# Turning q and k for attention: eight TensorE transposes and two PSUM copies a group, or a transposing DMA

## The chip, the cores and the metric

The kernel runs on one core of one Trainium2 chip. The metric is the device time of one launch in microseconds (us). Every kernel's time below is a median of several runs; every ratio compares runs in the fast state alone. Engines are called PE (TensorE), PEld (its weight loads), DVE (VectorE), ACT (ScalarE), POOL (GpSimd) and SP (SyncE, which here only issues DMAs). "Clock" is the TensorE clock that was granted, as a share of full speed.

## The reference, cut to what matters

A gated linear attention with a complex decay, then a gated feed-forward layer:

```python
for t in range(S):                                   # B=4, H=8, S=768, D=48
    S_re, S_im = a_re*S_re - a_im*S_im + kv[t], a_re*S_im + a_im*S_re
    y[:, :, t] = einsum('bhd,bhde->bhe', q[:, :, t], S_re)
x = y as (3072 tokens, 384)
out = x + sigmoid(x @ w_res) * ((gelu(x @ w_gate) * (x @ w_val)) @ w_out)    # d_ff = 1536
```

The kernel does the recurrence in chunks of 128 tokens. The decay becomes a scaling and a rotation of q and k by an angle for each token and element, so that each head has 48 real and 48 imaginary columns: 96. Within a chunk the attention matrix is K Q^T, masked. For that matmul q and k must lie with the 96 columns on the partitions; they are computed with the tokens on the partitions. So they have to be turned, 128 tokens x 96 columns for each head. The change is about who turns them.

## The kernel before

There are 12 groups of 256 tokens (two chunks c each, three groups for one batch element), and six units u of two groups. A unit passes through two stages:

- the *preparing stage* (`phase_x`): logarithms, exponentials, arctan, then the sines and cosines CS of the angles fg, for the next units; output matmuls of the unit before; some attention;
- the *gelu stage* (`phase_y`): twelve blocks of gate and value matmuls (gp, vp) with their gelu, the rotations of q and k, and nearly all attention of the next unit.

ACT changes its function table at each boundary, so the boundaries can be read from its table loads. Within a stage a scheduler lays down one static order for each engine; each engine then runs its own list in order, and waits where an operand is not there.

The parts that the change touches, with cuts marked:

```python
pE  = tile_pool(bufs=2)          # E, Ei and the angles fg: two of each
pQ  = tile_pool(bufs=2)          # CS, and the rotated Q and K
psT = tile_pool(bufs=1, PSUM)    # transposes
psA = tile_pool(bufs=1, PSUM)    # attention matrix
# ... cut
def cs_t(g, c):
    if c == 0:
        T["fg", g] = pE.tile([128, C * H, 2, D], FP, tag="fg")
    # ... matmul cst, r = round(cst)                        (DVE)
    fg[:, hs, 1, :] = cst - r                             # (DVE, 0.54 us a chunk)
    if c == C - 1:
        fg[:, :, 0, :] = abs(fg[:, :, 1, :])              # (DVE, 0.95 us)

def p2_sin(g):
    CS[:, :, 0] = Sin(2 pi * fg[:, :, 0] + hpi)           # (ACT, 0.94 us)
    CS[:, :, 1] = Sin(2 pi * fg[:, :, 1])                 # (ACT, 0.83 us)

def mk(nm, src):                                          # rotation, nm is "Q" or "K"
    t = pQ.tile([128, C * H, 2, D], BF, tag=nm)
    nc.vector.tensor_tensor(out=t, in0=T["CS", g], in1=sb, op=OP.mult)
# ... cut
def grp(hg):                                              # four heads of one chunk
    tp = psT.tile([128, 1024], BF, tag="tp")
    for j in range(4): nc.tensor.transpose(out=tp[0:DD, j*128:j*128+128], in_=Q(x), identity=ident)
    for j in range(4): nc.tensor.transpose(out=tp[0:DD, 512+j*128:640+j*128], in_=K(x), identity=ident)
    nc.scalar.copy(out=qk[0:DD, 0:512], in_=tp[0:DD, 0:512])              # Q, ACT
    nc.vector.tensor_copy(out=qk[0:DD, 512:1024], in_=tp[0:DD, 512:1024]) # K, DVE
    at = psA.tile([128, 4, 128], FP, tag="at")
    for j in range(4): nc.tensor.matmul(out=at[:, j], lhsT=qk[.. K ..], rhs=qk[.. Q ..])
    nc.vector.tensor_tensor(out=atm, in0=at, in1=mask4, op=OP.mult)
```

All loads of a_re, a_im, q and k, and all stores, are issued by SP, one after the other.

## Time and profile before

| | before |
|---|---|
| time, median of 3 runs | 343.38 us (342.88 to 344.42) |
| span of the profiled run | 341.4 us |
| up to the first gelu stage | 94.0 us |
| four preparing stages / four gelu stages | 80.0 / 104.5 us |
| rest (last attention, last gelu stage, output) | 62.9 us |

From the page of the kernel before, the busy time of the engines, the granted clock in 40 slices (a digit is tenths), and the DMA queue that SP feeds (packets, MB, share of 16 engines):

```profile
PE 267.3 (78%) x2054; PEld 160.6 (47%) x2080; DVE 245.4 (72%) x440; ACT 203.0 (59%) x338; POOL 67.1 (20%) x104
...
PEclk9996585559699999999999999999999999999999
...
q1 hardware_dynamic: 103296, 23.60, 40.6%
```

PE is the busiest, but 78% is an average over stages with different limits. The table of busy time by stretch for the kernel before shows them. Each line is a stage: its window, its length, busy time of each engine (with the count of instructions), the granted clock, the DMA share and GB/s. The lines are the first gelu stage, the first preparing stage after it, and the third gelu stage. (The DMA share adds up the packets' times and can exceed 1, as the 1.26 below.)

```profile
core 0: us, PE busy (x) PEld busy (x) DVE busy (x) ACT busy (x) POOL busy (x), PEclk, DMA share, GB/s
94.02:120.00 25.98, 24.39 (x251) 15.67 (x254) 22.43 (x40) 16.34 (x31) 6.08 (x8) 1.00 1.26 166
120.00:140.79 20.79, 17.26 (x83) 9.65 (x83) 16.21 (x32) 17.13 (x28) 6.58 (x10) 1.00 0.94 156
...
187.23:213.84 26.61, 26.06 (x269) 16.79 (x271) 24.28 (x44) 16.80 (x31) 0.00 (x0) 1.00 0.28 53
```

In the gelu stages PE is busy 94 to 99% of the time at full clock, with DVE close behind. PE work removed there should count. In the preparing stage shown no engine is above 84%: it is limited by a chain of small steps. Note also the DMA share: over 1 in the first gelu stage, where the loads are still running, 0.28 in the third.

What turning costs, from the groups of instructions of the kernel before (line, engine, operation, operands, count, then busy us and mean ns of one, then idle time before them):

```profile
L322 ACT COPY qk<-tp 96x512 bf16<-96x512 bf16 x48 | 27.9, 581 | 28.3 <-PE tp L320 15.1
...
L317 PE MATMUL tp<-ident,Q 128*96 128x128 bf16 x192 | 20.1, 231 | 13.4 <-DVE qk L323 8.6
...
L323 DVE COPY qk<-tp 96x512 bf16<-96x512 bf16 x48 | 19.9, 414 | 10.1 <-ACT qk L322 9.6
L119 ACT ACTIVATE CS<-fg,hpi 128x768 bf16<-128x768 f32 x12 | 11.2, 935 | 24.1 <-DVE fg L237 24.1
```

The 231 ns of a transpose overlaps its neighbours. The timeline of PE in the kernel before gives the real cost (start in us, duration, then the instructions of one row):

```profile
201.20 0.38 PE L317 MATMUL tp<-ident,Q 128*96 128x128 bf16 x4
201.42 0.39 PE L320 MATMUL tp<-ident,K 128*96 128x128 bf16 x4
201.64 0.33 PE L426 MATMUL rp<-wr,xT 128*128 128x384 bf16 x1
```

Four transposes hold PE for 0.22 us from start to start, so a group of four heads (q and k) costs 0.44 us of PE, 0.58 us of ACT and 0.41 us of DVE. There are 48 such groups.

The last line of the groups: ACT's sines wait 24.1 us in all for fg.

### The profile page before, as it was taken

The numbers are of one execution on the slowest core, as the hardware profiler recorded it, in microseconds if no ns is written. First come the engines' busy times: TensorE is split into PE (matmuls) and PEld (weight loads), VectorE is DVE, ScalarE is ACT, GpSimd is POOL, SyncE is SP. The second block draws the span as 40 slices with busy tenths as digits, with TensorE's granted clock in tenths as the row PEclk, the third lists the DMA queues.
The fourth block names the chain that finished last, engine by engine and source line by source line (L and its number), as shares of the span: only waits on it lengthen the run. The fifth ranks groups of instructions, "written<-read, shape, count | busy, mean of one in ns | idle before, by whom it ended". The sixth has DMA issues, their size and how long they took to land.

```text
span 341.4 us, 5552 instructions
## 1 busy us (share of the span) xinstructions
PE 267.3 (78%) x2054; PEld 160.6 (47%) x2080; DVE 245.4 (72%) x440; ACT 203.0 (59%) x338; POOL 67.1 (20%) x104
## 2 busy tenths in 40 slices
PE   0330544298689979899897999779999989999995
PEld 0110224275256545465554566445665556565452
DVE  1322696249999649999389998499994799855443
ACT  3365434349665696756896656977568275662530
POOL 9423710050522224102232000150001300000000
PEclk9996585559699999999999999999999999999999
DMA  9999999999999999527422620021000210002002
GB/s 139 136 139 175 176 184 196 175 170 171 155 167 162 169 133 172 109 46 72 25 63 54 118 46 2 2 48 47 3 2 1 50 46 2 0 2 92 2 1 92
DMA packets 135258, 30.25 MB, mean 89 GB/s; under 512 B 127168, under 2 KB 135232, under 8 KB 135232
## 3 DMA queue, kind: packets, MB, share of 16 engines
q1 hardware_dynamic: 103296, 23.60, 40.6%
q0 software_dynamic: 31936, 6.31, 21.9%
q8 instruction: 16, 0.26, 0.3%
q14 instruction: 10, 0.08, 0.1%
HBM read 31.33 MB, written 4.76 MB: 106 GB/s over the span
## 4 chain that ended last, share of the span: by engine, by line
PE 47%; DMA 18%; DVE 15%; ACT 9%; issue 7%; POOL 3%; ACTq 0%; DVEq 0%; POOLq 0%
PE vp L414 12%; PE gp L410 11%; PE op L434 6%; DMA dm_266<-ar 4%; DMA v<-in_v_dram 4%; PE tp L320 3%; PE at L327 3%; PE tp L317 3%; PE rp L426 3%; DMA dm_663<-Ei 2%; ACT L445 2%; DVE fg L237 2%; DVE r L234 2%; DMA dm_219<-ar 2%; ACT CS L119 2%
## 5 line engine op out<-in xcount | busy, mean ns | idle before, releaser
L410 PE MATMUL gp<-xT,wg 128*128 128x512 bf16 x196 | 61.5, 382 | 7.6 <-DVE xT L401 4.6
L414 PE MATMUL vp<-xT,wv 128*128 128x512 bf16 x210 | 60.3, 382 | 0.3
L322 ACT COPY qk<-tp 96x512 bf16<-96x512 bf16 x48 | 27.9, 581 | 28.3 <-PE tp L320 15.1
L180 DVE TENSOR_TENSOR ai<-s,ai 128x768 f32<-128x768 f32 x12 | 11.1, 955 | 38.5 <-ACT s L119 26.9
L330 DVE TENSOR_TENSOR atm<-at,mask_81 128x512 bf16<-128x512 f32 x48 | 32.8, 683 | 7.2 <-PE at L327 7.2
L410 PEld LDWEIGHTS <-wg 128*128 128x128 bf16 x216 | 20.0, 98 | 23.0 <-issue 8.9
L317 PE MATMUL tp<-ident,Q 128*96 128x128 bf16 x192 | 20.1, 231 | 13.4 <-DVE qk L323 8.6
L142 POOL DMA_DIRECT2D v<-in_v_dram x24 | 21.3, 902 | 43.0 <-PE y L367 22.4
L414 PEld LDWEIGHTS <-wv 128*128 128x128 bf16 x216 | 20.4, 98 | 19.3 <-issue 0.8
L317 PEld LDWEIGHTS <-Q 128*96 128x96 bf16 x192 | 17.3, 131 | 21.4 <-issue 10.0
L323 DVE COPY qk<-tp 96x512 bf16<-96x512 bf16 x48 | 19.9, 414 | 10.1 <-ACT qk L322 9.6
L203 PE MATMUL csl<-ar,lt0a 128*128 128x384 f32 x24 | 12.3, 601 | 18.6 <-DVE ar L189 18.5
L119 ACT ACTIVATE CS<-fg,hpi 128x768 bf16<-128x768 f32 x12 | 11.2, 935 | 24.1 <-DVE fg L237 24.1
L445 ACT ACT_TABLE_LOAD x18 | 23.1, 1283 | 1.0 <-PEq L547 0.7
L320 PE MATMUL tp<-ident,K 128*96 128x128 bf16 x192 | 22.1, 235 | 0.0
L227 PE MATMUL cst<-ai,lt0b 128*128 128x384 f32 x24 | 11.6, 568 | 13.4 <-ACT ai L119 13.1
L327 PE MATMUL at<-qk 96*128 96x128 bf16 x192 | 20.4, 228 | 0.1
L437 DVE SCALAR_TENSOR_TENSOR ot<-sg,op 128x384 f32<-128x384 f32 x24 | 13.2, 549 | 9.4 <-PE op L434 9.4
L365 PE MATMUL y<-v,atm 128*128 128x48 bf16 x192 | 17.9, 187 | 2.5 <-DVE atm L330 2.4
L365 PEld LDWEIGHTS <-atm 128*128 128x128 bf16 x192 | 13.5, 98 | 12.8 <-DVE atm L330 11.6
L320 PEld LDWEIGHTS <-K 128*96 128x96 bf16 x192 | 17.3, 133 | 0.0
L357 PEld LDWEIGHTS <-K 128*96 128x96 bf16 x160 | 13.3, 138 | 6.5 <-DVE K L292 4.2
(155 smaller groups left out, 626.3 us busy)
## 6 DMA issues: line engine op xcount, KB each, us to landing
ar<-in_a_re_dram SPq DMA_DIRECT2D x24, 192.0 KB, 5.7
ai<-in_a_im_dram SPq DMA_DIRECT2D x24, 192.0 KB, 5.5
q<-in_q_dram SPq DMA_DIRECT2D x24, 192.0 KB, 5.1
k<-in_k_dram SPq DMA_DIRECT2D x24, 192.0 KB, 5.0
out_dram<-ot SPq DMA_DIRECT2D x24, 192.0 KB, 1.9
v<-in_v_dram POOLq DMA_DIRECT2D x24, 96.0 KB, 6.3
wg<-in_moe_w_gate_dram POOLq DMA_DIRECT2D x4, 288.0 KB, 9.2
wv<-in_moe_w_val_dram POOLq DMA_DIRECT2D x4, 288.0 KB, 10.5
```

Source lines behind the costliest of these rows:

```text
L142: nc.gpsimd.dma_start(out=t[:, c], in_=rows(v, g, c))
L317: nc.tensor.transpose(out=tp[0:DD, j * 128:j * 128 + 128], in_=Q(x), identity=ident)
L320: nc.tensor.transpose(out=tp[0:DD, 512 + j * 128:640 + j * 128], in_=K(x), identity=ident)
L322: nc.scalar.copy(out=qk[0:DD, 0:512], in_=tp[0:DD, 0:512])
L323: nc.vector.tensor_copy(out=qk[0:DD, 512:1024], in_=tp[0:DD, 512:1024])
L327: nc.tensor.matmul(out=at[:, j], lhsT=qk[0:DD, 512 + j * 128:640 + j * 128], rhs=qk[0:DD, j * 128:j * 128 + 128], start=True, stop=True)
L330: nc.vector.tensor_tensor(out=atm, in0=at, in1=mask4, op=OP.mult)
L365: nc.tensor.matmul(out=ys, lhsT=st["atm", hg][:, j], rhs=V(h), start=True, stop=first)
L410: nc.tensor.matmul(out=gp, lhsT=wg[:, fi, ffi * 128:(ffi + 1) * 128], rhs=xT[:, fi, :], start=(fi == 0), stop=(fi == KD - 1))
L414: nc.tensor.matmul(out=vp, lhsT=wv[:, fi, ffi * 128:(ffi + 1) * 128], rhs=xT[:, fi, :], start=(fi == 0), stop=(fi == KD - 1))
L434: nc.tensor.matmul(out=ps, lhsT=h2[:, ffi, jj * 128:(jj + 1) * 128], rhs=wo[:, ffi, :], start=(ffi == 0), stop=(ffi == KF - 1))
L445: tab(nc.scalar.preload_act_table_set(nm))
```

## The change

The intent is to take the turning off PE, ACT and DVE. The rotated q and k are padded from 96 to 128 columns a head, and a DMA that transposes turns one chunk (8 heads, 128 x 1024 elements of two bytes, 256 KB) at a time, SBUF to SBUF. There are 40 of these, issued by SP right after the rotation. The first unit (g < 2) keeps the PE transposes. The padding needs SBUF, which is paid for with one buffer less for a_re/a_im, one less for q/k, and one fg instead of two. The freed PSUM bank doubles the buffer of the attention matrix. The diff, cut to its core:

```diff
-    lda = tile_pool(bufs=6)            # a_re, a_im
-    ldq = tile_pool(bufs=4)            # q, k
+    lda = tile_pool(bufs=5)
+    ldq = tile_pool(bufs=3)
+    pF = tile_pool(bufs=1)             # fg
+    pT = tile_pool(bufs=3)             # turned q and k
-    psT = tile_pool(bufs=1, PSUM)
-    psA = tile_pool(bufs=1, PSUM)
+    psA = tile_pool(bufs=2, PSUM)
+    Qb = [singles.tile([128, C * H, 128], BF) for i in range(2)]    # and Kb; columns 96.. set to 0 once
 ...
-            T["fg", g] = pE.tile(...)
+            T["fg", g] = pF.tile(...)
 ...
-                t = pQ.tile([128, C * H, 2, D], BF, tag=nm, name=nm)
-                nc.vector.tensor_tensor(out=t, in0=T["CS", g], in1=sb, op=OP.mult)
+                t = (Qb if nm == "Q" else Kb)[g % 2]
+                nc.vector.tensor_tensor(out=t[:, :, 0:DD]..., in0=T["CS", g], in1=sb, op=OP.mult)
+                if g >= 2:
+                    for c in range(C):
+                        tt = pT.tile([128, H, 128], BF, tag=nm + "T")
+                        nc.sync.dma_start_transpose(out=tt, in_=t[:, c * H:(c + 1) * H])
+                        T[nm + "T", g, c] = tt
 ...
-                (8 transposes, ACT copy of Q, DVE copy of K)
+                if g < 2:
+                    pe_transposes(hg)    # the same, through a psM bank
-                    nc.tensor.matmul(out=at[:, j], lhsT=qk[.. K ..], rhs=qk[.. Q ..])
+                    nc.tensor.matmul(out=at[:, j], lhsT=KT[0:DD, hg * 4 + j], rhs=QT[0:DD, hg * 4 + j])
```

More of the change, by code (lines that the diff above doesn't have):

```diff
@@ L85 @@
     wr = singles.tile([128, KD, DM], BF, name="wr")
-    lda = ctx.enter_context(tc.tile_pool(name="lda", bufs=6))
-    ldq = ctx.enter_context(tc.tile_pool(name="ldq", bufs=4))
+    lda = ctx.enter_context(tc.tile_pool(name="lda", bufs=5))
+    ldq = ctx.enter_context(tc.tile_pool(name="ldq", bufs=3))
     ldv = ctx.enter_context(tc.tile_pool(name="ldv", bufs=6))
@@ L92 @@
     pE = ctx.enter_context(tc.tile_pool(name="pE", bufs=2))
+    pF = ctx.enter_context(tc.tile_pool(name="pF", bufs=1))
     pQ = ctx.enter_context(tc.tile_pool(name="pQ", bufs=2))
     pK = ctx.enter_context(tc.tile_pool(name="pK", bufs=1))
+    pT = ctx.enter_context(tc.tile_pool(name="pT", bufs=3))
     sqp = ctx.enter_context(tc.tile_pool(name="sqp", bufs=2))
@@ L103 @@
     psM = ctx.enter_context(tc.tile_pool(name="psM", bufs=4, space=PSUM))
-    psT = ctx.enter_context(tc.tile_pool(name="psT", bufs=1, space=PSUM))
-    psA = ctx.enter_context(tc.tile_pool(name="psA", bufs=1, space=PSUM))
+    psA = ctx.enter_context(tc.tile_pool(name="psA", bufs=2, space=PSUM))
     psY = ctx.enter_context(tc.tile_pool(name="psY", bufs=1, space=PSUM))
     psD = ctx.enter_context(tc.tile_pool(name="psD", bufs=1, space=PSUM))
+    Qb = [singles.tile([128, C * H, 128], BF, name="Qb%d" % i) for i in range(2)]
+    Kb = [singles.tile([128, C * H, 128], BF, name="Kb%d" % i) for i in range(2)]
+    for t in Qb + Kb:
+        nc.gpsimd.memset(t[:, :, DD:128], 0.0)
     T = {}
@@ L223, in cs_t @@
         if c == 0:
-            T["fg", g] = pE.tile([128, C * H, 2, D], FP, tag="fg", name="fg")
+            T["fg", g] = pF.tile([128, C * H, 2, D], FP, tag="fg", name="fg")
         sl = slice(c * DM, (c + 1) * DM)
@@ L289, in x @@
             def x():
-                t = pQ.tile([128, C * H, 2, D], BF, tag=nm, name=nm)
+                t = (Qb if nm == "Q" else Kb)[g % 2]
                 sb = T[src, g].rearrange("p (x u d) -> p x u d", u=1, d=D).to_broadcast([128, C * H, 2, D])
-                nc.vector.tensor_tensor(out=t, in0=T["CS", g], in1=sb, op=OP.mult)
+                nc.vector.tensor_tensor(out=t[:, :, 0:DD].rearrange("p x (u d) -> p x u d", u=2), in0=T["CS", g],
+                                        in1=sb, op=OP.mult)
                 T[nm, g] = t
+                if g >= 2:
+                    for c in range(C):
+                        tt = pT.tile([128, H, 128], BF, tag=nm + "T", name=nm + "T")
+                        nc.sync.dma_start_transpose(out=tt, in_=t[:, c * H:(c + 1) * H].rearrange("p x e -> p (x e)"))
+                        T[nm + "T", g, c] = tt
             return x
@@ L301, in attention, with pe_transposes @@
         st = {}
-        def Q(x):
-            return T["Q", g][:, x].rearrange("p u d -> p (u d)")
-        def K(x):
-            return T["K", g][:, x].rearrange("p u d -> p (u d)")
         def V(h):
             return T["v", g][:, c, h]
+        def pe_transposes(hg):
+            if hg == 0:
+                for nm in ("Q", "K"):
+                    T[nm + "T", g, c] = pT.tile([128, H, 128], BF, tag=nm + "T", name=nm + "T")
+            tp = psM.tile([128, 2, 4, 128], BF, tag="mm", name="tp")
+            for i, nm in enumerate(("Q", "K")):
+                for j in range(4):
+                    nc.tensor.transpose(out=tp[0:DD, i, j], in_=T[nm, g][:, c * H + hg * 4 + j, 0:DD], identity=ident)
+            hs = slice(hg * 4, hg * 4 + 4)
+            nc.scalar.copy(out=T["QT", g, c][0:DD, hs], in_=tp[0:DD, 0])
+            nc.vector.tensor_copy(out=T["KT", g, c][0:DD, hs], in_=tp[0:DD, 1])
         def grp(hg):
             def a():
-                tp = psT.tile([128, 1024], BF, tag="tp", name="tp")
-                for j in range(4):
-                    x = c * H + hg * 4 + j
-                    nc.tensor.transpose(out=tp[0:DD, j * 128:j * 128 + 128], in_=Q(x), identity=ident)
-                for j in range(4):
-                    x = c * H + hg * 4 + j
-                    nc.tensor.transpose(out=tp[0:DD, 512 + j * 128:640 + j * 128], in_=K(x), identity=ident)
-                qk = sqp.tile([128, 1024], BF, tag="qk", name="qk")
-                nc.scalar.copy(out=qk[0:DD, 0:512], in_=tp[0:DD, 0:512])
-                nc.vector.tensor_copy(out=qk[0:DD, 512:1024], in_=tp[0:DD, 512:1024])
-                st["qk", hg] = qk
+                if g < 2:
+                    pe_transposes(hg)
+                QT, KT = T["QT", g, c], T["KT", g, c]
                 at = psA.tile([128, 4, 128], FP, tag="at", name="at")
                 for j in range(4):
-                    nc.tensor.matmul(out=at[:, j], lhsT=qk[0:DD, 512 + j * 128:640 + j * 128],
-                                     rhs=qk[0:DD, j * 128:j * 128 + 128], start=True, stop=True)
+                    nc.tensor.matmul(out=at[:, j], lhsT=KT[0:DD, hg * 4 + j], rhs=QT[0:DD, hg * 4 + j],
+                                     start=True, stop=True)
                 atm = sqp.tile([128, 4, 128], BF, tag="atm", name="atm")
@@ L356, in dk @@
             for h in range(H):
-                nc.tensor.matmul(out=d[0:DD, h * D:(h + 1) * D], lhsT=K(c * H + h), rhs=V(h),
+                nc.tensor.matmul(out=d[0:DD, h * D:(h + 1) * D], lhsT=T["K", g][:, c * H + h, 0:DD], rhs=V(h),
                                  start=(c == 0 and h == 0), stop=(h == H - 1), skip_group_check=True)
@@ L366, in yy @@
                 if not first:
-                    nc.tensor.matmul(out=ys, lhsT=st["qk", hg][0:DD, j * 128:j * 128 + 128],
+                    nc.tensor.matmul(out=ys, lhsT=T["QT", g, c][0:DD, h],
                                      rhs=T["Gbf"][0:DD, h], start=False, stop=True)
```

## The prediction

> **What bounds the kernel.** Span 341.4 us. The page's busy shares are PE 78%, DVE 72%, ACT 59%, but the busy table by stretch shows two regimes. Up to 96 us PE is busy only 42 us: granted clock 0.60 to 0.85, DMA engines saturated by loads, and the chain of waits runs through small decay DMAs (13.9 and 8.4 us for 1.5 KB). From then each unit has a preparing stage of 19 to 22 us (logarithms, arctan, sin; the chain alternates DVE fg and ACT CS) and a gelu stage of 24 to 26 us, with PE busy 95 to 98% and DVE 85 to 92% (188.5 to 214 us: PE 24.95, DVE 23.01, ACT 15.69 of 25.5). Nearly all attention, hence the transposes, runs in the gelu stages. There PE, closely followed by DVE, is the limit.
>
> **Removed** (40 of 48 four-head groups). PE: in the timeline four transposes take 0.22 us from start to start (busy time, 231 ns each, overlaps), so 0.44 us a group, 17.7 us in all, 3.5 us per gelu stage. ACT copies 40 x 0.581 = 23.2 us; DVE copies 40 x 0.414 = 16.6 us, 3.3 us per stage. The handover PE, ACT and DVE, PE before the attention matmul goes too, and that matmul's PSUM gets two buffers.
>
> **Added.** 40 DMA transposes of 256 KB, 10.5 MB. The Trainium skill ("DMA: Bandwidth & Descriptors", Latency and other measured facts) gives 261 GB/s effective for a DMA transpose; I estimate 1 us each plus about 2 us fixed, 40 us of transfer in all (this trace shows none). All issuing queues share the same 16 engines, the page says; the trace agrees (1.5 KB took 13.9 us behind loads). So they should land in 3 to 5 us where DMA is nearly idle (after 150 us, share 0.03 to 0.39), in 6 to 10 us in the first gelu stage, which still has saturated loads. Rotations write a stride of 128 instead of 96: I expect 948 ns unchanged.
>
> **Moved.** fg single-buffered: the second group's fg waits for the first's sin (2.05 us of fg writes, partly hidden): I estimate 1 us more per preparing stage. One q/k and one a buffer less: loads come later but run over a unit ahead, so little.
>
> **Sum.** Of 3.5 us per gelu stage about 3 are kept, five times: -15. Single fg +5; first gelu stage waiting for late transposes +3; later stages +1; PSUM and handover relief -3. About -10: **332 us**, range 320 to 346. Faster by over 2% 0.62, within 2% 0.28, slower 0.10.
>
> **What would show it.** Landing times of 3 to 5 us after 150 us; gelu stages of 22 to 23 us, PE still over 90% busy and DVE near 20 us; preparing stages 1 us longer with ACT CS waiting longer for fg; PE waiting on a turned tile in the first gelu stage; rotations near 948 ns; the hardware queue's DMA share up 10 to 15 points.
>
> **What would make it wrong.** A transpose of 3 us or more on all 16 engines (120 us in all), putting attention on DMA latency in every stage and throttling loads; the in-order SP queue holding a transpose behind a store or load that waits; PE waiting in order for a turned tile with gelu matmuls behind it; attention pushed into the next stage; or the rotation losing DVE's speed (10 us more if it halves).

## More of the kernel before

The timeline of ACT at the end of one preparing stage, for its two groups (in brackets the idle time before, and what ended it):

```profile
182.81 0.94 ACT L119 ACTIVATE CS<-fg,hpi 128x768 bf16<-128x768 f32 x1 [2.04 <-DVE fg L237]
...
185.54 0.94 ACT L119 ACTIVATE CS<-fg,hpi 128x768 bf16<-128x768 f32 x1 [1.06 <-DVE fg L237]
```

The second group's sine starts 2.73 us after the first's.

## The result, and the profile after

| | before | after |
|---|---|---|
| time, median of 4 runs, same rounds | 343.73 us (342.88 to 344.42) | 366.64 us (364.33 to 367.15) |
| ratio | | 1.0655, 95% interval 1.0602 to 1.0708 |

The kernel became 6.6% slower, where some 3% faster (332 us) was predicted. All ratios in this document are the mean time of one kernel's fast runs over the mean of the other's fast runs in the same rounds, so they are not quite the ratio of the medians quoted. Executions over 1.5% slower than the fastest of the same kernel are left out of the means.

The page of the kernel after, the same rows:

```profile
PE 262.4 (72%) x1760; PEld 146.2 (40%) x1760; DVE 233.9 (64%) x400; ACT 182.6 (50%) x298; POOL 69.2 (19%) x108
...
PEclk9955685599659899889899989999789999999998
...
q1 hardware_dynamic: 145536, 34.09, 53.5%
```

ACT and DVE did lose their copies, and the DMA share rose by 13 points. But PE lost only 4.9 us of busy time where 17.7 us of work was removed, and the row of the clock shows one reason: after 94 us it was at full speed in every stage before, and it has many 7s and 8s now. Busy time in a slowed stretch is longer (an example stands under e4).

The same three stages by stretch, for the kernel after:

```profile
94.32:132.17 37.85, 25.49 (x185) 14.10 (x185) 17.51 (x28) 12.48 (x22) 3.54 (x4) 0.74 0.98 132
132.17:157.09 24.92, 18.48 (x79) 9.91 (x78) 16.17 (x32) 17.13 (x27) 6.28 (x10) 0.89 0.70 120
...
209.57:234.91 25.34, 22.80 (x198) 12.72 (x197) 19.64 (x33) 12.47 (x23) 0.00 (x0) 0.93 0.61 113
```

All stages, in us, read in the same way. Their differences add up to the whole: 24.0 us between the two profiled spans, 341.4 and 365.4.

| stage | before | after | after - before |
|---|---|---|---|
| start | 94.0 | 94.3 | +0.3 |
| gelu 0 | 26.0 | 37.9 | +11.9 |
| preparing 1, 2, 3, 4 | 20.8, 20.1, 20.7, 18.5 | 24.9, 23.3, 22.2, 19.0 | +9.4 together |
| gelu 1 | 26.4 | 29.2 | +2.8 |
| gelu 2 | 26.6 | 25.3 | -1.3 |
| gelu 3 | 25.5 | 27.3 | +1.8 |
| rest | 62.9 | 61.9 | -0.9 |

So there are two places to explain: the first gelu stage, and the preparing stages. And one disappointment: the later gelu stages gain 1.3 us at best, where 3 us were predicted.

**The first gelu stage.** Four extracts of the timeline of the kernel after, first PE, then SP ("SPq", what its queue was busy issuing), then DVE:

```profile
97.49 1.06 PE L426 MATMUL vp<-xT,wv 128*128 128x512 bf16 x2
105.30 1.04 PE L339 MATMUL at<-QT,KT 96*128 96x128 bf16 x8 [6.75 <-DMA KT<-Kb_154]
```

```profile
95.19 2.59 SPq L139 DMA_DIRECT2D ai<-in_a_im_dram  x2
97.83 0.74 SPq L139 DMA_DIRECT2D ar<-in_a_re_dram  x1
98.68 3.05 SPq L306 DMA_TRANSPOSE QT<-Qb_152  x2
101.86 2.65 SPq L306 DMA_TRANSPOSE KT<-Kb_154  x2
```

```profile
92.52 0.95 DVE L300 TENSOR_TENSOR Kb_154<-CS,kE 128x1536 bf16<-128x1536 bf16 x1
```

K's rotation ended at 93.5 us. SP was still issuing the loads of a_re and a_im, which take it 0.7 to 1.3 us each here, then it issued the two transposes of Q, and only at 101.86 us the first transpose of K. That landed at 105.3. PE, which runs its list in order, had come to the attention matmul at 98.5 and stood for 6.75 us, with gate and value matmuls behind it. The groups of instructions show such waits over the whole run (11.3 us for this K buffer, and 7.1 us more for the other), and the growth of ACT's wait for fg:

```profile
L339 PE MATMUL at<-QT,KT 96*128 96x128 bf16 x192 | 21.1, 247 | 19.0 <-DMA KT<-Kb_154 11.3
...
L127 ACT ACTIVATE CS<-fg,hpi 128x768 bf16<-128x768 f32 x12 | 11.2, 935 | 34.6 <-DVE fg L245 34.6
```

The DMA issues show that the transposes themselves were not slow in the median (count, median us from issue to landing; the slowest of K's took 7.4 us):

```profile
QT<-Qb_152 SPq DMA_TRANSPOSE x10, 3.3
KT<-Kb_154 SPq DMA_TRANSPOSE x10, 3.3
```

**The preparing stages.** The timeline of ACT, then of DVE, at the end of the same preparing stage as the one shown of before:

```profile
203.31 0.94 ACT L127 ACTIVATE CS<-fg,hpi 128x768 bf16<-128x768 f32 x1 [3.42 <-DVE fg L245]
...
207.88 0.94 ACT L127 ACTIVATE CS<-fg,hpi 128x768 bf16<-128x768 f32 x1 [2.90 <-DVE fg L245]
```

```profile
205.01 1.02 DVE L243 TENSOR_TENSOR fg<-cst,r 128x384 f32<-128x384 f32 x2
205.95 0.15 DVE L282 TENSOR_TENSOR M<-M,m_1211 96x8 f32<-96x8 f32 x1
206.03 0.95 DVE L300 TENSOR_TENSOR Qb_152<-CS,qE 128x1536 bf16<-128x1536 bf16 x1
206.90 0.95 DVE L245 SCALAR_TENSOR_TENSOR fg<-fg 128x768 f32<-128x768 f32 x1
```

The second sine now starts 4.57 us after the first, not 2.73. With one fg the second group's fg may be written only after the first group's sines have read it (they end at 204.98; the write starts at 205.01). So the whole sequence, two writes and the absolute value, stands between the two sines; and in DVE's order a rotation of 0.95 us stands in the middle of it. That this is the cause is so far a reading; the experiments test it.

### The profile page after: what moved, and what is told of

Its sections match the earlier page's. It is cut to its first block, busy times and chain, and to the rows that moved or that the text cites. A ratio compares the mean times of both kernels' runs of the same rounds, so it can differ in the third digit from the quotient of the medians.

```text
span 365.4 us, 4880 instructions
## 1 busy us (share of the span) xinstructions
PE 262.4 (72%) x1760; PEld 146.2 (40%) x1760; DVE 233.9 (64%) x400; ACT 182.6 (50%) x298; POOL 69.2 (19%) x108
## 3 DMA queue, kind: packets, MB, share of 16 engines
q1 hardware_dynamic: 145536, 34.09, 53.5%
q0 software_dynamic: 31936, 6.31, 20.7%
## 4 chain that ended last, share of the span: by engine, by line
PE 33%; DMA 19%; SPq 14%; DVE 14%; issue 10%; ACT 7%; POOL 2%; DVEq 0%; ACTq 0%; POOLq 0%
SPq L139 12%; PE vp L426 8%; PE gp L422 7%; DMA KT<-Kb_155 6%; PE op L446 6%; DMA KT<-Kb_154 5%; PE at L339 3%; DMA q<-in_q_dram 3%; ACT CS L127 2%; PE rp L438 2%; DVE fg L245 2%; DVE fg L243 2%; DVE ar L196 1%; ACT L457 1%; PE y L377 1%
## 5 line engine op out<-in xcount | busy, mean ns | idle before, releaser
L422 PE MATMUL gp<-xT,wg 128*128 128x512 bf16 x216 | 65.0, 398 | 7.6 <-ACT h_783 L127 2.1
L426 PE MATMUL vp<-xT,wv 128*128 128x512 bf16 x216 | 66.0, 403 | 0.0
L339 PE MATMUL at<-QT,KT 96*128 96x128 bf16 x192 | 21.1, 247 | 19.0 <-DMA KT<-Kb_154 11.3
L127 ACT ACTIVATE CS<-fg,hpi 128x768 bf16<-128x768 f32 x12 | 11.2, 935 | 34.6 <-DVE fg L245 34.6
L339 PEld LDWEIGHTS <-KT 96*128 96x128 bf16 x192 | 15.5, 112 | 27.6 <-DMA KT<-Kb_154 14.1
L457 ACT ACT_TABLE_LOAD x18 | 23.1, 1283 | 1.0 <-PEq L559 0.7
L235 PE MATMUL cst<-ai,lt0b 128*128 128x384 f32 x24 | 11.6, 570 | 15.0 <-ACT ai L127 14.7
L382 ACT CAST x<-y 128x384 bf16<-128x384 f32 x24 | 11.4, 477 | 14.9 <-PE y L379 9.5
L379 PEld LDWEIGHTS <-QT 96*128 96x128 bf16 x160 | 11.7, 102 | 14.9 <-issue 13.4
L127 ACT ACTIVATE h_783<-gp 128x512 bf16<-128x512 f32 x12 | 7.1, 597 | 19.8 <-PE gp L422 19.7
L127 ACT ACTIVATE sg<-rp 128x384 f32<-128x384 f32 x24 | 11.7, 491 | 8.3 <-PE rp L438 7.4
L438 PE MATMUL rp<-wr,xT 128*128 128x384 bf16 x72 | 15.7, 336 | 0.1
L379 PE MATMUL y<-Gb,QT 96*128 96x48 bf16 x160 | 15.6, 191 | 0.0
```

Of the source, the lines that this page charges most:

```text
L127: tab(nc.scalar.activation(**kw))
L339: nc.tensor.matmul(out=at[:, j], lhsT=KT[0:DD, hg * 4 + j], rhs=QT[0:DD, hg * 4 + j], start=True, stop=True)
L379: nc.tensor.matmul(out=ys, lhsT=T["QT", g, c][0:DD, h], rhs=T["Gbf"][0:DD, h], start=False, stop=True)
L422: nc.tensor.matmul(out=gp, lhsT=wg[:, fi, ffi * 128:(ffi + 1) * 128], rhs=xT[:, fi, :], start=(fi == 0), stop=(fi == KD - 1))
L426: nc.tensor.matmul(out=vp, lhsT=wv[:, fi, ffi * 128:(ffi + 1) * 128], rhs=xT[:, fi, :], start=(fi == 0), stop=(fi == KD - 1))
L438: nc.tensor.matmul(out=rp, lhsT=xT[:, fi, jj * 128:(jj + 1) * 128], rhs=wr[:, fi, :], start=(fi == 0), stop=(fi == KD - 1))
```

## The experiments

Theories at the start:

- **Single fg**: the preparing stages, and part of the rest, are lost to the one fg buffer.
- **Waiting for turned tiles**: PE in its order stands for KT. Why KT is late has rivals: the traffic of the transposes slows everything; K is the last product to be rotated, so it has too little slack; SP issues it behind loads and behind Q (queue order); or PE's list simply puts the attention matmul too early, so that PE stands there whatever the queue does.
- **Other parts of the edit** (padding, fewer load buffers, first unit's transposes through another PSUM pool) cost something by themselves.

The expectations use short names for these. Sixteen kernels were run, all of them correct. The kernel before was run beside them in four batches, with medians of 343.75 (first four), 345.67 (next four), 343.55 (next four) and 343.15 us (last four). The second of these holds two slow runs of seven; its fast runs have a median of 344.46 us. Each batch ran on another chip, so between batches the ratios say more than the microseconds.

### e1: everything but the DMA transposes

```diff
-                if g >= 2:      # DMA transposes
+                if g >= NG:     # never
-                if g < 2:       # PE transposes
+                if g < NG:      # always
```

> The changed kernel with every unit turned by TensorE: no DMA transpose at all, but all that was moved stays (single fg, fewer load buffers, padded q and k, PSUM split). Theory WAIT (the loss is PE standing in order for turned tiles and the half clock after it): gelu stages back to 25 to 26 us at clock 1.0, only the longer preparing stages stay; 346 us, 342 to 352. Rival MOVED (buffers and PSUM are the loss): 357 us or more.

Measured: 350.0 us, ratio 1.0178 (1.0122 to 1.0233). So without any turning by DMA the rest of the edit still costs 6 us. Turning by DMA adds about 17 us to that (366.64 less 350.0, from different rounds).

### e2: e1, with the DMA transposes running into tiles that nobody reads

```diff
+    pD = tile_pool(bufs=1)
+                if g >= 2:  # besides the PE transposes, which are used
+                    tt = pD.tile([128, H, 128], BF, tag=nm + "D")
+                    nc.sync.dma_start_transpose(out=tt, in_=t[:, c * H:(c + 1) * H])
```

> As e1, and the 40 DMA transposes are issued as in the changed kernel, into tiles that nothing reads. Theory WAIT: the transfers cost little when nothing waits for them, within 5 us of e1, no PE wait on a turned tile. Rival TRAFFIC (the SP queue and the 16 engines are crowded, loads and decay DMAs come late): 10 us or more above e1, near 360.

Measured: 349.79 us, ratio 1.0176 (1.0125 to 1.0227), level with e1. All 40 transposes run, take their share of the DMA engines and of SP's queue, and cost nothing that these runs can tell (the intervals are half a percent to either side). The theory that their traffic is the cost falls. What is left is that somebody waits for them.

### e3: DMA transposes from the third unit on

```diff
-                if g >= 2:
+                if g >= 4:
-                if g < 2:
+                if g < 4:
```

> DMA transposes only from the third unit on (32 of 40). Theory WAIT: the first gelu stage, 37.9 us against 26.0, goes back to about 26 us, so 354 us, 350 to 358. If the cost were the same per transpose in every stage, a fifth of the 23 us goes: 362 us.

Measured: 353.48 us, ratio 1.0279 (1.0217 to 1.0341): 13 us less than the changed kernel, though only 8 of its 40 transposes went back to PE. In its profile gelu 0 took 25.0 us, where it took 37.9, but gelu 1 took 28.4, where turning by DMA now begins. PE's waits for KT fell to 8.8 us in all.

### e4: the changed kernel with two fg buffers

```diff
-    pF = tile_pool(bufs=1)
+    pF = tile_pool(bufs=2)
```

> The changed kernel with fg double-buffered again. If the single fg made the preparing stages longer (4.1, 3.2, 1.5, 0.5 us), about 9 us go: 357 us. If those stages are longer for late DMAs or the order alone, nothing goes: 364 to 367 us.

Measured: 350.77 us, ratio 1.0193 (1.0136 to 1.025). One word of the edit is worth 16 us of the 23 lost. Its four preparing stages sum to 80.1 us, against 80.0 before and 89.4 after. ACT's waits (us in all, times, longest), in e4:

```profile
ACT CS L127 <- DVE fg L245: 22.7, 12, 5.7
```

That is the 24.1 us of the kernel before, not the 34.6 us of after. Of the 16.1 us between the two profiled spans (365.4 and 349.3), 9.3 lie in the preparing stages, 2.8 in gelu 0, 2.4 in gelu 3 and 1.7 in the start. What e4 still loses against the kernel before is in the gelu stages, by stretch (the first and the third):

```profile
92.62:127.64 35.02, 24.08 (x195) 13.38 (x196) 19.46 (x31) 12.45 (x22) 5.60 (x7) 0.87 1.21 152
...
198.90:224.05 25.15, 22.33 (x205) 12.64 (x206) 21.80 (x36) 12.37 (x22) 0.00 (x0) 1.00 0.78 140
```

Here is the answer to the disappointment. In the third gelu stage PE's work fell from 26.06 to 22.33 us, by 3.7 us, about what was predicted; but the stage shortened only from 26.61 to 25.15, since PE was no longer the limit throughout. PE's waits within this stage of e4:

```profile
PE at L339 <- DMA KT<-Kb: 2.1, 2, 1.7
PE gp L422 <- ACT h L127: 0.6, 1, 0.6
```

So 2.1 us of the relief went straight into standing for KT. In e4 such waits take 10.8 us in gelu 0, 4.1 in gelu 1, 2.1 in gelu 2 and 2.5 in gelu 3, and 21.2 us in the whole run. That is more than the 17.7 us of PE work that the change removed.

In gelu 0 there is one thing more: the work of 24.08 us is no shorter than before, 24.39, although some 3.5 us were removed. The first wait of e4 is from 97.9 to 105.1 us. The clock around it, by stretch:

```profile
101.00:103.00 2.00, 0.00 (x0) 0.00 (x0) 0.00 (x0) 0.00 (x0) 0.00 (x0) 0.69 1.18 219
...
105.00:107.00 2.00, 1.89 (x11) 1.28 (x12) 0.92 (x2) 0.00 (x0) 0.00 (x0) 0.50 0.95 175
107.00:109.00 2.00, 2.00 (x17) 0.95 (x16) 0.98 (x2) 0.60 (x1) 0.00 (x0) 0.60 1.23 171
109.00:111.00 2.00, 1.94 (x34) 1.29 (x32) 1.93 (x4) 1.02 (x2) 0.00 (x0) 1.00 0.89 178
```

The clock fell to half during the wait and stayed there for about 3.5 us of matmuls after it. The first eight attention matmuls after each of three waits show what that costs: 1.03 us where the clock had gone to 0.50, 0.62 us where it had not (in brackets the wait):

```profile
105.11 1.03 PE L339 MATMUL at<-QT,KT 96*128 96x128 bf16 x8 [7.25 <-DMA KT<-Kb]
120.55 0.62 PE L339 MATMUL at<-QT,KT 96*128 96x128 bf16 x8 [3.52 <-DMA KT<-Kb]
...
170.65 1.03 PE L339 MATMUL at<-QT,KT 96*128 96x128 bf16 x8 [2.70 <-DMA KT<-Kb]
```

The Trainium skill ("TensorE: Matmul & The Clock Gate", section "HAM oscillation — how this bites in real kernels") gives the rule of no idle gap of PE above about 3.4 us. As a threshold this trace does not bear it out: the wait of 7.25 us lost the clock and the one of 3.52 us did not, but the one of 2.70 us in gelu 1 did (0.50 from about 170.0 to 176.7 us). Nor is every slow stretch the work of a wait for a turned tile: e4 came into gelu 0 at 0.50 and ran so until 94.9 us, and in the changed kernel the clock fell at about 93.7 us, before the wait of 6.75 us, and came back at 110.8. So a wait can be paid twice, once while PE stands and once while it runs slowly; how long a gap the clock allows is not shown here.

### e5: e1 with two fg buffers

```diff
 (e1)
-    pF = tile_pool(bufs=1)
+    pF = tile_pool(bufs=2)
```

> e1 (no DMA transpose) with the double fg of e4. Theory FG (the single fg costs about 9 us in the preparing stages and that is all that was lost among the moved parts): 350.0 minus 9 is 341 us, 338 to 344, level with or just under the kernel before. Rival: other moved parts (fewer load buffers, padded q and k, PSUM split) carry part of the 6 us of e1: 345 us or more.

Measured: 344.91 us, ratio 1.0001 (0.9938 to 1.0065). With two fg buffers and no DMA turning the edit is level with the kernel before, within 0.7%. So the padding, the fewer load buffers and the moved PSUM banks cost nothing measurable together, and the 6 us of e1 were the single fg. What e4 loses (350.77) against e5 is the DMA turning alone: about 6 us, where it was to gain 10 or more.

### e6: e4, with the loads of the first gelu stage held back

```diff
 (e4)
-        for g in gs(u + 3): load_a(g)               # before phase_y
+        if u != 0: for g in gs(u + 3): load_a(g)
         phase_y(u)
+        if u == 0:
+            with tc.issue_after(<last transpose of K of group 2>):
+                for g in gs(u + 3): load_a(g)
```

> e4 with the a loads of the fourth unit held on the SP queue until the K transposes of the first group of the first gelu stage stand before them. Theory QUEUE (of the 12 us from the rotated K to its use in that stage about 5 us are spent behind load issues on the in-order SP queue): the first PE wait falls from 7.25 us to about 2 to 3 us, gelu0 from 35.0 to about 30 us, total 346 us. Rival ENGINES (the DMA engines are full, so the transposes land late whatever stands before them on the queue): gelu0 stays at 33 us or more, total 349 to 351 us.

Measured: 349.28 us over four runs, of which the first, the profiled one, was slow; the three fast ones are 347.31, 347.73 and 350.83; ratio 1.0125 (1.0037 to 1.0212). In its profile, which is of the slow run and is therefore only an indication, SP issued K's transposes 5.3 us earlier (96.59 us, where e4 has 101.84) and the first wait was 3.03 us, where e4's is 7.25. So it did what it was made for, and the order in SP's queue probably sets when KT lands in this stage. But by the fast runs the gain is about 2 us (the ratio fell from 1.0193 to 1.0125, with overlapping intervals), less than expected.

### e7: only Q by DMA, two fg buffers

```diff
 (e4)
-                if g >= 2:
+                if g >= 2 and nm == "Q":      # K: PE transposes and DVE copy, as before
```

> e4 with only Q turned by DMA; K is turned by TensorE and copied by VectorE as before. Theory WAIT: Q is rotated a few us ahead of K, so its transpose hides, and PE no longer waits for a turned tile after the first gelu stage; half the PE relief stays: gelu stages 24 to 25 us, first one under 30 us, total 338 us, 334 to 343. If it is the number of transposes or their traffic that costs, about half of the 7 us of e4 stays: 346 us or more.

Measured: 338.71 us, ratio 0.9844 (0.9779 to 0.9909). Half of the relief, and faster than before. PE waits 0.7 us in all for a turned tile. Gelu 0 is 22.3 us, at a clock of 1.00.

### e8: e3 with two fg buffers

```diff
 (e3)
-    pF = tile_pool(bufs=1)
+    pF = tile_pool(bufs=2)
```

> e4 with DMA transposes from the third unit on only. Theory: e3 and e4 add up, 353.5 minus about 9 to 10 for fg: 343 us, 340 to 346; gelu0 25 us, gelu1 about 28 us with PE still waiting for K tiles, preparing stages 20 to 21 us.

Measured: 343.23 us, ratio 0.9972 (0.9916 to 1.0027). The loss in gelu 0 is gone (23.1 us), but gelu 1 takes 29.5 us, longer than before's 26.4. The longest stage is now the first whose unit is turned by DMA, as in e3. Against e4 7.5 us are won.

### e9: the mirror of e7, only K by DMA

```diff
 (e4)
-                if g >= 2:
+                if g >= 2 and nm == "K":      # Q: PE transposes and ACT copy, as before
```

> Mirror of e7: only K is turned by DMA, Q by TensorE with its ScalarE copy; as many DMA transposes as in e7, double fg. Theory SLACK (what costs is how late the operand is rotated before its use; K is rotated last): PE waits on K tiles as in e4, first gelu stage 30 us or more, total 346 to 352 us. Rival NUMBER (half the transposes, half the trouble, whichever operand): as e7, 338 to 340 us.

Measured: 338.85 us, ratio 0.9872 (0.9827 to 0.9917), level with e7. There is one wait for KT, of 3.7 us, in gelu 0. The theory that K is the trouble, being rotated last (346 us or more), falls: either operand alone may come by DMA. But K's wait is not free: in the profiled run, the slowest of the four, gelu 0 took 28.3 us at a clock of 0.86, where e7 has 22.3 at 1.00.

### e10: the kernel before, with a single fg buffer

```diff
+    pF = tile_pool(bufs=1)
-            T["fg", g] = pE.tile([128, C * H, 2, D], FP, tag="fg", name="fg")
+            T["fg", g] = pF.tile([128, C * H, 2, D], FP, tag="fg", name="fg")
```

> The kernel before with nothing changed but the single fg. Theory FG: the second sin waits for the second fg in each preparing stage, 1 to 2.5 us a stage: 350 us, 347 to 354. If fg costs only together with DMA transposes: 343 to 345 us.

Measured: 357.39 us over four runs, of which one (359.97) was slow; the three fast ones are 353.92, 356.85 and 357.92; ratio 1.0362 (1.0304 to 1.042). The buffer alone, put into the kernel before with nothing else, costs 12.5 us (mean of the fast runs, 356.2 against 343.8). The same wait, in e10:

```profile
ACT CS L120 <- DVE fg L238: 36.1, 11, 7.0
```

Its four preparing stages sum to 88.0 us, against 80.0. The cost is not confined to them: gelu 0 and gelu 3 are 2.3 and 1.7 us longer too. In the kernels where some of the attention spills into the preparing stages (e1 and e5, and the half-turned kernels) the single fg costs less, 5 to 6 us.

### e11: e7, with the copy of K on ACT

```diff
 (e7)
-            nc.vector.tensor_copy(out=T["KT", g, c][0:DD, hs], in_=tp[0:DD, 1])
+            (nc.vector.tensor_copy if g < 2 else nc.scalar.copy)(out=T["KT", ...], in_=tp[0:DD, 1])
```

> e7 with the K copy on ScalarE instead of VectorE. In e7's gelu stages DVE is busy 20.7 of 22.3 us, ACT 11.5, PE 21.6 at full clock. If DVE limits beside PE, gelu stages fall by about 1 us and preparing stages by 0.5 us: 333 us. If PE alone limits: 338 us, unchanged.

Measured: 337.4 us (336.17 to 338.18), ratio 0.9811 (0.9783 to 0.9839). Perhaps 1 us better than e7, within the intervals.

### e12: e7 with a single fg

```diff
 (e7)
-    pF = tile_pool(bufs=2)
+    pF = tile_pool(bufs=1)
```

> e7 with the single fg of the change: only Q turned by DMA, everything else as changed. If the two losses are separate, the single fg costs 6 to 9 us here too: 345 us, 343 to 349; if it costs only where PE also waits for K tiles: 339 us.

Measured: 344.13 us, ratio 0.9996 (0.9963 to 1.0029). The single fg takes 5.4 us, all that the half turning had won.

### e13: e7, with K also turned by DMA into tiles that nobody reads

```diff
 (e7)
+    pD = tile_pool(bufs=2);  xp: bufs 10 -> 9 for room
-                if g >= 2 and nm == "Q":
+                if g >= 2:
-                        tt = pT.tile(...)
+                        tt = (pT if nm == "Q" else pD).tile(...)
```

> e7 (Q by DMA, K by TensorE) plus the 20 K transposes of e4, issued in their place into tiles that nothing reads (one x buffer less, to make room). As many transposes as e4. If the number of transfers costs: near e4, 347 to 351 us. If only standing for a tile that lands late costs: as e7, 337 to 341 us, since no one waits for the K tiles; Q's own transposes of the next group may come slightly later.

Measured: 336.94 us, ratio 0.9805 (0.9757 to 0.9852). All transposes of e4 run in e4's order, and the kernel is 14 us faster than e4. So neither their number, their traffic nor their hold on SP makes e4 slow by itself. What differs is that no matmul waits for K's transposes, and that in PE's list K's own transposes now stand before the attention; these two were not separated.

### e14: e9, with Q also turned by DMA into tiles that nobody reads

```diff
 (e9)
+    (as e13: Q's transposes stand before K's in SP's queue, unread)
```

> e9 (K by DMA, Q by TensorE) plus the 20 Q transposes into tiles that nothing reads, issued before K's on the same queue. Theory QUEUE ORDER (the needed tile lands late because the other operand's two transposes, 1.3 us each, stand before it): PE waits for K tiles return, 344 to 350 us. If the K tiles have slack enough: as e9, 338 to 341 us.

Measured: 341.79 us, ratio 0.9959 (0.9917 to 1.0). If the place of K behind Q in the queue were the main cause, 344 us or more was expected. It costs up to 3 us against e9. KT is waited for only once, 4.4 us, in gelu 0, which takes 28.0 us (28.3 in e9).

### e15: e4, with the attention placed later in PE's order

```diff
 (e4)
+                    if g >= 2 and g % 2 == 0 and c == 0:
+                        (first attention matmuls stand after the vp matmuls of the 7th gelu block)
-        weave((0.0, 1.0, gv), (0.0, 0.4, pr), (0.3, 0.95, att_steps(u + 1, 0)))
+        weave((0.0, 1.0, gv), (0.0, 0.4, pr), (0.55, 1.0, att_steps(u + 1, 0)))      # u >= 0
```

> e4 with the attention of the unit's first group forced behind the seventh gelu block in PE's order (and emitted later), so that PE has 9 us of gelu matmuls before it first needs a turned tile. Theory STAND (PE stands in order with work left behind the wait): PE's waits on K tiles fall from 21 us to under 8, gelu0 from 35 to about 28 us, total 343 us, 339 to 346. If the loss is the DMA traffic itself, or the attention pushed later costs as much elsewhere: 349 us or more.

Measured: 344.89 us, ratio 1.0065 (1.0009 to 1.0121). That is about 5 us better than e4 (4.4 by the ratios, 5.9 by the medians of different rounds), without touching a single DMA. PE's waits for turned tiles fell from 21.2 to 11.6 us (9.6 on KT, 2.0 on QT). So the place of the attention in PE's list is a cause, and its effect is bigger than the 2 us of e6. But the first gelu stage hardly moved:

```profile
92.31:125.49 33.18, 28.38 (x197) 15.36 (x195) 19.43 (x31) 12.28 (x22) 5.21 (x7) 0.77 1.26 156
```

It was expected near 28 us. PE stood far less (busy 28.38 of 33.18), but at a clock of 0.77 the same work took 28.38 us, where e4 took 24.08. The trace shows when it was low, though not why:

```profile
103.43 0.62 PE L339 MATMUL at<-QT,KT 96*128 96x128 bf16 x8 [1.94 <-DMA KT<-Kb]
110.44 0.23 PE L339 MATMUL at<-QT,KT 96*128 96x128 bf16 x1 [1.74 <-DMA KT<-Kb]
...
112.00:121.00 9.00, 7.88 (x52) 4.04 (x52) 3.08 (x6) 2.52 (x5) 3.17 (x4) 0.50 1.22 153
```

About 1 us after each of these two waits ended, the clock fell to 0.50, for 3.4 us and then for 10.2 us (111.3 to 121.5). Both waits are shorter than the one of 3.52 us that e4 came through at full clock.

### e16: e11, with K by DMA too for the second group of each later unit

```diff
 (e11)
-                if g >= 2 and nm == "Q":
+                if g >= 2 and (nm == "Q" or (g >= 4 and g % 2 == 1)):
```

> e11 with K by DMA too for the second group of each unit from the third unit on, where e4 shows PE waiting only 0.2 to 0.4 us in two of three stages. PE is relieved of another 1.8 us per unit: 333 us, 331 to 336. If PE waits for those tiles again: 338 us or more.

Measured: 337.25 us, ratio 0.9813 (0.9767 to 0.9858), level with e11. The second group of a unit has a stage more of time before its attention, and PE waits only 0.8 us in all for turned tiles. But more turning by DMA won nothing more.

### The best versions

e13, e16 and e11 (336.9, 337.3 and 337.4 us) cannot be told apart. Each is 1.9% under the kernel before, with an interval that excludes 1 but reaches to both sides of 2%. e11 is the simplest: Q by DMA, K by PE with ACT's copy, two fg buffers.

### What was not tried, and what stays open

- The clock's part of the loss is read from the traces only; no run held the clock up while PE waited.
- That in e4's first gelu stage part of the cost is placement (e15), part landing (e6, e8) and part clock is shown; how the rest of e15's gelu 0, 33.2 us against 26.0 before, divides is not.
- That either operand alone makes the kernel faster, and both together are about 12 us slower than that, is shown as a fact (e7, e9, e13, e14 against e4). Why is not shown. The reading is that where PE must transpose one operand first, its list has other work of the same group ahead of the attention matmul and spreads attention further: about 170 PE instructions lie in gelu 0 of e7, e9 and e11, 195 in e4, and the others' preparing stages hold about 60 more than e4's (e5, where PE turns everything, has this spread too). e15 supports this reading. It does not prove that nothing else differs.

## Why the prediction was wrong, point by point

**Right.** The bounds: PE at 94 to 99% in the gelu stages. Transposes of 3 to 5 us: 3.2 to 3.3 us in the median (in the first gelu stage, where 6 to 10 us were predicted, the medians of the four buffers were 3.3 to 6.9 us, so landing was rather faster there than predicted). The rotations, with the wider stride, 944 to 952 ns against 948 expected. The hardware queue's DMA share up 10 to 15 points: 40.6 to 53.5%. PE waiting for a turned tile in the first gelu stage. DVE near 20 us in a later gelu stage: 19.64. And, in "What would make it wrong", "PE waiting in order for a turned tile with gelu matmuls behind it": that is what happened, along with SP holding a transpose behind other issues.

**Wrong: "Single fg +5".** The mechanism was right and the size was not. It was costed as 1 us more in each preparing stage, the fg writes being "partly hidden". Measured: 12.5 us alone (e10), 16 us in the changed kernel (after to e4), and 1.5 to 4.1 us in each of the first three preparing stages. The estimate counted the writes of fg and forgot what stands between them in DVE's static order. In the trace the two sines came to lie 4.57 us apart, where they were 2.73, and the first sine waits longer as well. With 12.5 or 16 us in the place of 5, the predicted sum of -10 becomes -2.5 or +1.

**Wrong: "First gelu stage waiting for late transposes +3".** The mechanism was right again, the size was not: +9.0 us in e4 (26.0 to 35.0), +11.9 in the changed kernel. The prediction looked at the landing time of one transpose. What counts is when it is issued: 8 us after K was rotated, behind loads and Q's transposes in SP's queue. To that comes the slower clock: in e4, of this stage's PE work, about 2.3 us before the wait and 3.5 us after it ran at 0.50.

**Wrong: "Of 3.5 us per gelu stage about 3 are kept, five times: -15" with "later stages +1".** This step failed in its logic, not only in its size. PE's work in the third gelu stage did fall by 3.7 us (e4), but only 1.5 us were kept, since 2.1 us became waits for KT. The gains of gelu 2, gelu 3 and the rest of the run sum to 3.6 us in e4 (1.46, 0.67 and 1.5), and gelu 1, which was counted among the gains, lost 3.8. PE busy 95% of a stage was read as "work removed is time won". It is true only if what replaces the work arrives before PE reaches it in order.

**Unneeded or not seen: "PSUM and handover relief -3".** e4 shows no place where it could be found. A gain of this size may hide in the half-turned kernels, and was not measured by itself.

With sizes from e10 and e4 the sum closes roughly. In e4, about -17.7 us of PE work removed, +21.2 us of waits for KT, and an estimate of +6 us of slower clock in the first two gelu stages (PE busy 24.1 and 25.0 us there, where before's 24.4 and 25.7 less 3.5 would be 20.9 and 22.2) give +9.5, against +7.9 us between the spans (341.4 and 349.3). The clock itself says about the same: some 5.8 us of PE work at 0.50 in each of the two stages, of which half is lost. This is an account from the traces, not an experiment. The single fg adds 16 us more.

## What to carry to other kernels

Moving work from an engine to a DMA swaps a cost in time for a latency in that engine's fixed order: before counting the relief, find for the first and the last user where it stands in its engine's list, when the issuing queue will get to the transfer, and what stands behind it. Transfers that nobody waits for were free here, forty of them in e2; the same transfers, waited for in order, took back more than they had relieved. And a buffer given up to make room has to be costed as its own change, by running it alone: here it was the larger part of the loss.

## What the Trainium skill lacked or had wrong

- "DMA: Bandwidth & Descriptors" (Latency and other measured facts) gives 261 GB/s effective for a DMA transpose with a non-contiguous middle dimension, 350 to 400 contiguous. For SBUF to SBUF transposes of 256 KB two rough estimates come out lower. Two of K's issued together held SP's queue for 2.65 us, 1.3 us each, or about 200 GB/s if the queue's time is taken for the transfer's; and the added share of the hardware queue (53.5% of 365.4 us less 40.6% of 341.4 us, over 40) is 1.4 us each, about 185 GB/s.
- No page says for this chip how long a transpose of a given size holds the issuing queue (the page above has cycle counts for it only in its part on trn3, without a tile size), though that helped to decide when K's landed: 1.2 to 2.1 us for each of K's in the changed kernel, 1.3 in the median, and loads of 192 KB ahead of them 0.7 to 1.3 us each. The same page's section "Issuing engines are not separate DMA queues" calls the sequencer's time "usually small relative to the DMA itself"; here 1.3 us of issue stood against 3.3 us from issue to landing.
- "VectorE: DVE Perf Modes" (The three transpose paths) compares single 128x128 blocks: 390 ns on TensorE, 1309 ns by DMA. One after another both come cheaper. Four TensorE transposes of 128x96 started 0.22 us apart, 55 ns each at full clock (and the PSUM copies, 0.58 and 0.41 us for four, cost more than the transposes), and a DMA turned eight blocks in 1.3 us of queue and 3.3 us from issue to landing.
- "TensorE: Matmul & The Clock Gate" (HAM oscillation — how this bites in real kernels) sets about 3.4 us as the idle gap to avoid. Here gaps on both sides of it did the opposite: a wait of 3.52 us kept the clock (e4), while waits of 2.70 us (e4), 1.94 and 1.74 us (both e15) came with 0.50 for 3.4 to 10.2 us. What decides was not found.
